# Attention and a feed-forward block on one Trainium2 core: the feed-forward by 1024 tokens, both projections by a 26-product scheme, weight forms made during attention

## The chip, the cores and the metric

One core of one Trainium2 chip runs the whole program in a single launch. The metric is the device time of that launch in microseconds (us). A run differs from the next by some tenths of a us, so about 0.2% (2 us) is what a measurement of this kernel can tell from no change.

## The reference, cut to what matters

```python
# q, k, v: (4, 8, 768, 64) float32; centroids: (8, 16, 64)
q_assign = argmax(normalised q @ normalised centroids.T)   # per head; the same for k
mask     = q_assign[..., :, None] == k_assign[..., None, :]
scores   = where(mask, q @ k.T / 8, -1e9)
x        = softmax(scores) @ v                             # -> (3072 tokens, 512)
h        = x @ w_in                                        # w_in (512, 2048)
g        = h * erf(softplus(h))
out      = g @ w_out                                       # w_out (2048, 512), all float32
```

## The kernel before, in words

**Attention** goes by 16 *periods*, one for each pair of heads of a batch entry. `period(p, i)` is one of six steps of period `p`; it handles two *units*, a unit being one block of 128 keys against one half (384) of the queries of both heads. `InOrder` keeps every engine's instructions in the order in which the program writes them, so what stands in the text first runs first on its engine.

In each step PE computes, for a unit half a period ahead, the scores from which the row maxima are taken (`maxima_step`: tile `wide`, the only one of its kind, filled by `kv,qv` and `km,qm`); DVE reduces it to `nmx` and so frees it. PE computes the scores proper into `sc`, ACT turns them into `pr` by an exponential, PE multiplies `pr` by v into `turned` (`attend`), and POOL adds the `pr` of one half up (`accumulate`, tile `more_out`, 128x768; five adds per half). At the steps 0 and 3 the half before is finished (`divide`): PE multiplies the sum by `minus`, ACT takes its inverse, DVE scales and writes a piece of x, and SP's queue stores it to `x_dram`. DVE also transposes q and k (`transposes`: k after step 2, q after step 5) and chooses the clusters (`choose`).

Beside that the weights pass through: 32 pieces of 128x512 are loaded (`fetch`) and rebuilt by ACT (`size`, `rest`, `sign`), DVE (`bounded`, `shifted`) and POOL (`summed`); 22 of them during periods 0 to 11, 10 *late* ones in the feed-forward. The same list runs in `period`: where `FORMS` says so, DVE takes a weight form (a sum or difference of two blocks of a weight, 128x512), and POOL one at steps 1 and 4 of periods 12 to 15.

```python
FORMS = {12: {0: 1}, 13: {0: 1}, 14: {0: 1, 3: 1}, 15: {0: 1, 3: 2, 4: 2, 5: 2}}
POOL_FORMS = range(12, 16)
```

**The feed-forward** goes by chunks of 512 tokens, six of them. `hidden` computes h for half of the hidden features at a time by a scheme with 7 products in place of 8 (`block`: each product is two matmuls of 128x128 by 128x256 into one of eight PSUM tiles, `bank` or `turned`; DVE and ACT add it to its places in `g`). The gate is Softplus and Erf on ACT and a product on DVE. The first chunk's out-projection (`project`) has 7 products as well; in the five others (`project26`) it has 26 products of four matmuls in place of 32, with forms of w_out that POOL makes once (`EARLY_FORMS`, `LATE_FORMS`), 10 of which lie in DRAM and are streamed through a ring of three tiles. The forms of x for the next chunk (`right_forms`) are made by DVE.

Of the kernel before, what the change touches and what calls it, by code (L numbers as in the profile page):

```python
# [19 lines left out]
P = 128  # L20
# [15 lines left out]
HT, HK, HF, HM = CT // 2, DM // P // 2, NFT // 2, DM // 2  # L36
FG = HF // 2
# [4 lines left out]
FORMS = {12: {0: 1}, 13: {0: 1}, 14: {0: 1, 3: 1}, 15: {0: 1, 3: 2, 4: 2, 5: 2}}  # L42
POOL_FORMS = range(12, 16)
# [9 lines left out]
KAPPA = {1: (0, 1), 2: (0, 0), 0: (1, 1), 3: (1, 0)}  # L53
EARLY_FORMS = [
    (-6, -4, -6, -1, None), (11, -2, -8, -1, None), (1, -3, -5, -1, None), (2, -6, 1, 1, None),
    (0, -4, 11, -1, 7), (8, -7, 11, -1, 8), (9, -5, -6, -1, 3), (11, -2, 11, 1, 10),
    (8, -7, 11, -1, 11), (6, -1, -5, 1, 1), (9, -1, 8, 1, 9), (8, 1, 11, -1, 4),
]
LATE_FORMS = [
    (3, -6, 0, -1, None), (4, 0, 6, -1, None), (0, -7, 0, 1, 6), (7, -3, 0, -1, None),  # L60
    (10, -4, 2, -1, 0), (6, -6, 6, -1, None), (9, -2, 6, 1, 2), (8, -7, 1, -1, 5),
]
HOME = (4, 0, 2, 3, 1, 5)
LAG = 1
RIGHT = [
    2, 7, -3, 100, -6, 3, 101, 4, -1, 102, 6, 103, 0,
    104, -4, -7, 105, 1, 106, 5, 107, -1, 108, -2, -2, 109,
]
# [5 lines left out]
    (-3, 16, 2, 10, 1), (-3, 17, 9, 16, 1), (-1, 18, 1, 17, 1), (2, 17, 6, 14, -1), (3, 6, 5, 6, 1),  # L74
# [35 lines left out]
N_STREAM = 10  # L110
RING = 3
KEPT = {0: 10, 5: 11}
HELD = 11
# [19 lines left out]
def kernel(  # L133
# [28 lines left out]
    more_in = const.tile([P, 3, HK, DFF // 2], F32, name="more_in")  # L162
    more_out = const.tile([P, 3, HF, HM], F32, name="more_out")
    x_more = const.tile([P, 3, HK, HT], F32, name="x_more")
    minus = const.tile([P, Q], F32, name="minus")
    alleps = const.tile([P, 1], F32, name="alleps")
    x_dram = dram.tile([DM, B * S], F32, name="x_dram")

# [30 lines left out]
    def part_of(i, lo, n):  # L199
        return more_out[:, i].rearrange("p f m -> p (f m)")[:, lo : lo + n]  # L200
# [78 lines left out]
    for f in range(HF):  # L279
        for g in (f, HF + f):  # L280
            w_steps.append((w_out[:, g], moe_w_out[g * P : (g + 1) * P]))
# [337 lines left out]
    def left_forms(engine, a11, a12, a21, a22, new):  # L619

        return [
            functools.partial(plus_of, new[0], a21, a22, engine),
            functools.partial(minus_of, new[1], new[0], a11, engine),
            functools.partial(minus_of, a21, a11, a21, engine),
            functools.partial(minus_of, new[2], a12, new[1], engine),
        ]

    def right_forms(engine, b11, b12, b21, b22, new):

        return [  # L630
            functools.partial(minus_of, new[0], b12, b11, engine),
            functools.partial(minus_of, new[1], b22, new[0], engine),
            functools.partial(minus_of, b12, b22, b12, engine),
            functools.partial(minus_of, new[2], new[1], b21, engine),
        ]

    def lefts(a11, a12, a21, a22, new):
        return {1: a11, 2: a12, 3: new[2], 4: a22, 5: new[0], 6: new[1], 7: a21}

    def rights(b11, b12, b21, b22, new):  # L640
        return {1: b11, 2: b21, 3: b22, 4: new[2], 5: new[0], 6: new[1], 7: b12}

    def w_in_parts(f, n):
        c1, c2 = slice(f * P, (f + n) * P), slice((HF + f) * P, (HF + f + n) * P)
        return (
            w_in[:, 0:HK, c1], w_in[:, HK:, c1], w_in[:, 0:HK, c2], w_in[:, HK:, c2],
            [more_in[:, i, :, c1] for i in range(3)],
        )

    def x_parts(n):  # L650
        x = x_of[n]
        return (
            x[:, 0:HK, 0:HT], x[:, 0:HK, HT:], x[:, HK:, 0:HT], x[:, HK:, HT:],
            [x_more[:, i] for i in range(3)],
        )

    def w_out_parts(f, n):
        f1, f2 = slice(f, f + n), slice(HF + f, HF + f + n)
        return (
            w_out[:, f1, 0:HM], w_out[:, f1, HM:], w_out[:, f2, 0:HM], w_out[:, f2, HM:],  # L660
            [more_out[:, i, f1] for i in range(3)],
        )

    g_of = {}
    sums_of = {}

    def g_parts(n, s, lot):
        g, new = g_of[n, s, lot], sums_of[n, s, lot]
        return (
            g[:, 0, :, 0:P], g[:, 1, :, 0:P], g[:, 0, :, P:], g[:, 1, :, P:],  # L670
            [new[:, i] for i in range(3)],
        )

    ORDER = (1, 2, 6, 7, 5, 3, 4)
    aside_work = []
    n_banks = [0]
    banks = [None]

    def bank():
        n_banks[0] += 1  # L680
        b = banks[n_banks[0] % len(banks)]
        if b is None:
            b = psb.tile([P, 512], F32, name="bank")
        return b[:, 0:HT]

    def onto(out, m, engine=ve):
        plus_of(out, m, out, engine)

    def fresh(c11, c12, c21, c22, first=ae.copy):
        return {  # L690
            1: [lambda m: first(out=c12, in_=m)],
            2: [lambda m: plus_of(c11, m, c12)],
            6: [lambda m: onto(c12, m)],
            7: [lambda m: plus_of(c21, m, c12)],
            5: [lambda m: onto(c12, m), lambda m: plus_of(c22, m, c21)],
            3: [lambda m: onto(c12, m)],
            4: [lambda m: minus_of(c21, c21, m)],
        }

    def further(c11, c12, c21, c22, u):  # L700
        return {
            1: [lambda m: ae.copy(out=u, in_=m), lambda m: onto(c11, m)],
            2: [lambda m: onto(c11, m)],
            6: [lambda m: onto(u, m), lambda m: onto(c12, u)],
            7: [lambda m: onto(u, m), lambda m: onto(c21, u)],
            5: [lambda m: onto(c12, m), lambda m: onto(u, m), lambda m: onto(c22, u)],
            3: [lambda m: onto(c12, m)],
            4: [lambda m: minus_of(c21, c21, m)],
        }

    def block(pieces, after, done=lambda i: None, pace=1):

        for i in ORDER:
            m = bank()
            pairs_of = pieces(i)
            for k, (lhsT, rhs) in enumerate(pairs_of):
                te.matmul(m, lhsT=lhsT, rhs=rhs, start=(k == 0), stop=(k == len(pairs_of) - 1))
            for f in after[i]:
                f(m)
            done(i)  # L720
            for work in aside_work[:pace]:
                work()
            del aside_work[:pace]

    def finish_aside():
        for work in aside_work:
            work()
        aside_work.clear()

    def hidden(n, lot, between={}, pace=1, **kw):  # L730

        for s in range(2):
            g_of[n, s, lot] = gp.tile([P, 2, FG, HT], F32, name="g")
        x = rights(*x_parts(n))
        for j in range(FG):
            w = lefts(*w_in_parts(lot * FG + j, 1))
            a, b = (g_of[n, s, lot] for s in range(2))
            block(
                lambda i: [(w[i][:, k], x[i][:, k]) for k in range(HK)],
                fresh(a[:, 0, j], b[:, 0, j], a[:, 1, j], b[:, 1, j], **kw), pace=pace,  # L740
            )
            between.get(j, lambda: None)()

    def gate(n, lot, s):

        g = g_of[n, s, lot].rearrange("p h j t -> p (h j t)")
        box = []

        def curves():
            t = actp.tile([P, 2 * FG * HT], F32, name="a_s")  # L750
            box.append(t)
            ae.activation(out=t, in_=g, func=ACT.Softplus)
            ae.activation(out=t, in_=t, func=ACT.Erf)

        def product(i):
            c = slice(i * 512, (i + 1) * 512)
            ve.tensor_tensor(out=g[:, c], in0=box[0][:, c], in1=g[:, c], op=ALU.mult)

        return curves, [functools.partial(product, i) for i in range(2 * FG * HT // 512)]

    def add_hidden(n, lot, s):
        sums_of[n, s, lot] = gsp.tile([P, 3, FG, P], F32, name="g_more")
        return left_forms(ve, *g_parts(n, s, lot))

    def idle(n):
        return [lambda: None] * n

    def gates(n, lot, which=(0, 1), between=()):
        work = list(between)
        for s in which:  # L770
            curves, products_of = gate(n, lot, s)
            if s == which[0]:
                work = [curves] + work + idle(7 - len(work)) + products_of
            else:
                work += [curves, *sums, *idle(3)] + products_of
            sums = add_hidden(n, lot, s)
        return work + sums
# [536 lines left out]
```

## Time and profile before

| what | value |
|---|---|
| three timed runs | 977.44, 977.89 and 978.01 us; median 977.89 |
| profiled execution, first to last instruction | 976.0 us; no time of its own is given beside the span, so the 1.9 us around it are taken from the median |
| granted TensorE clock | 1.000 |
| PE / PEld / DVE / ACT / POOL busy | 99% / 74% / 78% / 54% / 42% |
| 302 to 408 us (periods 12 to 15): PE, DVE, POOL busy of 106 | 106.0, 85.4, 89.2 us |
| 408 to 560 us (first of the feed-forward): PE, DVE, ACT, POOL busy of 151.9 | 151.9, 125.1, 77.0, 95.9 us |
| 560 to 976 us: PE, DVE, ACT, POOL busy of 416 | 411.9, 290.6, 162.0, 0 us |
| DMA | 88.4 MB, 91 GB/s in the mean |

How to read it: the span is cut by engine. PE is TensorE's matmuls and PEld its weight loads, DVE is VectorE, ACT ScalarE, POOL GpSimd, SP the queue that issues DMAs. All instructions but a few carry the line of one helper (L124), so groups are told apart by tiles (output<-inputs) and shapes. A number in square brackets behind a row is idle time of the engine before it, with what ended it. In the chain of work that ended last each row is a start, a length, an engine and how many instructions. An f32 matmul leaves two records.

### The profile page before, as it was taken

The numbers are of one execution on the slowest core, as the hardware profiler recorded it, in microseconds if no ns is written. First come the engines' busy times: TensorE is split into PE (matmuls) and PEld (weight loads), VectorE is DVE, ScalarE is ACT, GpSimd is POOL, SyncE is SP. The second block draws the span as 40 slices with busy tenths as digits, with TensorE's granted clock in tenths as the row PEclk, the third lists the DMA queues.
The fourth block names the chain that finished last, engine by engine and source line by source line (L and its number), as shares of the span: only waits on it lengthen the run. The fifth ranks groups of instructions, "written<-read, shape, count | busy, mean of one in ns | idle before, by whom it ended". The sixth has DMA issues, their size and how long they took to land.

```text
span 976.0 us, 20840 instructions
## 1 busy us (share of the span) xinstructions
PE 967.6 (99%) x8282; PEld 723.8 (74%) x8282; DVE 758.8 (78%) x1432; ACT 526.7 (54%) x799; POOL 410.0 (42%) x277
## 2 busy tenths in 40 slices
PE   8999999999999999999999999999999999999998
PEld 3555555555555555688888888888888888888887
DVE  8888888888888886879788786568666856685766
ACT  3777777777777665377613430562155235413541
POOL 1688887788888888853199600000000000000000
PEclk9999999999999999999999999999999999999999
DMA  9444444444444211142004543023302320131023
GB/s 226 74 109 110 108 110 109 107 110 109 87 110 110 54 35 34 50 149 87 0 22 173 194 147 135 1 65 130 108 0 87 130 87 1 65 139 57 1 86 108
DMA packets 157185, 88.42 MB, mean 91 GB/s; under 512 B 129696, under 2 KB 139424, under 8 KB 157088
## 3 DMA queue, kind: packets, MB, share of 16 engines
q1 hardware_dynamic: 154592, 86.67, 31.5%
q8 instruction: 65, 1.06, 0.4%
q10 hardware_dynamic: 2496, 0.43, 0.2%
q14 instruction: 32, 0.26, 0.1%
HBM read 68.19 MB, written 18.87 MB: 89 GB/s over the span
## 4 chain that ended last, share of the span: by engine, by line
PE 97%; DVE 2%; DMA 0%; issue 0%; ACT 0%; DVEq 0%; SPq 0%
PE bank L124 43%; PE turned L124 32%; PE sc L124 17%; PE wide L124 6%; DVE nmx L124 1%; DMA in_q<-in_q_dram 0%; DVE kT L124 0%; DVE sims L124 0%; DVE qT L124 0%; DVE km L124 0%; DVE turned L124 0%; DVE nbig L124 0%; ACT qm L124 0%; DVE ccT L124 0%; DVE osb L124 0%
## 5 line engine op out<-in xcount | busy, mean ns | idle before, releaser
L124 POOL TENSOR_TENSOR more_out<-more_out,pr 128x768 f32<-128x768 f32 x128 | 217.2, 1697 | 18.5 <-ACT pr L124 10.0
L124 DVE TENSOR_REDUCE nmx<-wide 128x2 f32<-128x768 f32 x189 | 180.5, 955 | 47.8 <-PE wide L124 47.0
L124 ACT ACTIVATE pr<-sc 128x768 f32<-128x768 f32 x192 | 148.7, 810 | 94.1 <-PE wide L124 77.2
L124 PE MATMUL turned<-pr,in_v 128*32 128x193 f32 x3072 | 144.8, 330 | 0.0
L124 DVE TENSOR_TENSOR g<-bank,g 128x256 f32<-128x256 f32 x222 | 89.4, 419 | 54.2 <-PE bank L124 34.1
L124 PEld LDWEIGHTS turned<-pr,in_v 128*32 128x32 f32 x3072 | 91.5, 109 | 50.7 <-issue 21.3
L124 DVE TENSOR_TENSOR g<-g 128x512 f32<-128x512 f32 x114 | 78.9, 692 | 42.3 <-PE bank L124 32.2
L124 PE MATMUL bank<-x_own,w_in 128*128 128x256 f32 x424 | 104.5, 379 | 0.0
L124 PE MATMUL sc<-qT,kT 64*128 64x384 f32 x528 | 98.3, 486 | 0.0
L124 PEld LDWEIGHTS bank<-x_own,w_in 128*128 128x128 f32 x424 | 80.4, 190 | 11.5 <-issue 0.6
L124 ACT ACT_TABLE_LOAD x48 | 61.6, 1283 | 38.2 <-DVE g L124 37.5
L124 DVE TENSOR_TENSOR g<-a_s,g 128x512 f32<-128x512 f32 x96 | 74.1, 786 | 3.2 <-ACT a_s L124 3.2
L124 PE MATMUL bank<-x_more,more_in 128*128 128x256 f32 x296 | 76.0, 379 | 0.0
L124 PE MATMUL bank<-w_out,g 128*128 128x256 f32 x328 | 75.7, 379 | 0.0
L124 POOL TENSOR_TENSOR more_out<-pr,pr 128x768 f32<-128x768 f32 x32 | 60.3, 1886 | 28.3 <-ACT pr L124 28.3
L124 PE MATMUL bank<-g_more,g 128*128 128x256 f32 x296 | 69.9, 379 | 0.0
L124 PEld LDWEIGHTS bank<-w_out,g 128*128 128x128 f32 x328 | 62.2, 190 | 8.6
L124 PEld LDWEIGHTS <-qv 64*128 64x128 bf16 x384 | 27.0, 93 | 52.9 <-issue 36.7
L124 PEld LDWEIGHTS sc<-qT,kT 64*128 64x128 f32 x528 | 50.0, 187 | 21.4 <-ACT inv L124 2.4
L124 PE MATMUL wide<-kv,qv 64*128 64x384 bf16 x378 | 64.0, 328 | 1.3 <-DVE nmx L124 0.6
L124 PE MATMUL wide<-km,qm 64*128 64x384 bf16 (+1 forms) x378 | 62.6, 327 | 0.0
L124 PEld LDWEIGHTS bank<-g_more,g 128*128 128x128 f32 x296 | 56.2, 190 | 7.6
(195 smaller groups left out, 1745.6 us busy)
## 6 DMA issues: line engine op xcount, KB each, us to landing
g_more<-b_dram SPq DMA_DIRECT2D x48, 512.0 KB, 3.2
x_own<-in_moe_w_in_dram SPq DMA_DIRECT2D x13, 512.0 KB, 4.1
in_v<-in_v_dram SPq DMA_DIRECT2D x32, 192.0 KB, 3.1
x_dram<-more_out SPq DMA_DIRECT2D x128, 48.0 KB, 1.8
x_own<-x_dram SPq DMA_DIRECT2D x6, 1024.0 KB, 5.5
in_k<-in_k_dram SPq DMA_DIRECT2D x59, 96.0 KB, 2.6
in_q<-in_q_dram SPq DMA_DIRECT2D x58, 96.0 KB, 2.6
out_dram<-osb SPq DMA_DIRECT2D x20, 256.0 KB, 3.2
```

The costliest lines, as they stand in the source:

```text
L124: ins = getattr(self.engine, name)(*args, **kw)
```

## The change

The feed-forward goes by 1024 tokens, three times. Each of the two projections is 26 products of eight matmuls (128x128 by 128x256). One product of `hidden` fills two PSUM banks (128x1024), and three such tiles are in use in turn; adds, copies and gate steps go by 128x1024. The list `HIDDEN` gives the products of the in-projection in order: the form or raw block of w_in, the form of x, and what is done with the result (an entry of one number is a copy on ACT, one of four an add on DVE, with -1 for the product itself).

The 18 forms of w_in are made during attention in two pieces of 128x512 each, in turn by DVE and POOL (`FORMS_VE`, `FORMS_GE`: period, then steps), and each is stored to DRAM; six raw blocks are stored too. In the feed-forward the blocks come back through a ring of five tiles in order of use; the place of w_in holds blocks of h then. The forms of x are made by POOL (`X_FORMS`: the first number is the product behind which it is issued, negative ones in the round before). The ten late weight pieces are spread over products 0 to 14 of the first round (`LATE_STEPS`), and the 18 forms of w_out are made by POOL there, behind the products that `OUT_MADE` names (26 and more are products of the out-projection); ten of them are stored and streamed in the later rounds. `SOFT`, `ERF` and `TIMES` place the gate.

```diff
-FORMS = {12: {0: 1}, 13: {0: 1}, 14: {0: 1, 3: 1}, 15: {0: 1, 3: 2, 4: 2, 5: 2}}
-POOL_FORMS = range(12, 16)
+W_FORMS = [
+    (17, -3, -5, -1, 4), (11, -6, -5, -1, 0), (6, -1, -5, 1, 3), (10, -6, 6, -1, 2), (9, -2, 10, 1, 1),
...
+W_RAW = {5: (0, 1), 7: (2, 3), 9: (5, 6)}
+FORMS_VE = {
+    9: {1: 1, 2: 1}, 10: {1: 1, 2: 1}, 11: {1: 1, 2: 1}, 12: {1: 1, 2: 1}, 13: {1: 1, 2: 1},
+    14: {1: 1, 2: 1, 3: 1, 4: 1}, 15: {0: 1, 1: 1, 2: 1, 3: 1, 4: 1, 5: 1},
+}
+FORMS_GE = {9: (0, 3), 10: (0, 3), 11: (0, 3), 12: (0, 1, 3, 4), 13: (0, 1, 3, 4), 14: (0, 1, 3, 4), 15: (0, 1, 3, 4)}
...
+X_FORMS = [
+    (-3, 0, 2, 4, -1), (-1, 1, 7, 1, 1), (-1, 2, 5, -2, -1), (2, 3, 7, 6, 1), (3, 2, -1, -2, -1), (4, 1, -2, 6, 1),
+    (5, 4, 5, 4, 1), (7, 2, -2, 0, 1), (9, 0, 5, -1, -1), (10, 1, 3, -1, -1), (11, 2, 0, 4, -1), (12, 3, 7, 3, 1),
+    (12, 4, -3, -4, -1), (14, 0, -3, 6, 1), (15, 1, -4, 6, 1), (16, 4, -2, 2, 1), (19, 0, -3, 5, -1), (20, 1, -1, 1, 1),
+]
+HIDDEN = [
+    (25, -1, [(0,)]),
+    (-2, 3, [(1,)]),
...
+    (-4, 1, [(13,), (9, 9, -1, -1), (14, 9, 3, -1), (9, 6, 9, 1), (12, 12, 9, -1), (3, 9, 3, -1)]),
+    (13, -1, [(15, -1, 10, -1), (8, 8, 15, -1)]),
...
+    (10, -5, [(18, -1, 17, -1)]),
...
+    (7, -2, [(6, -1, 6, -1), (18, 6, 18, -1)]),
...
+OUT_MADE = {
+    14: [17], 16: [22], 18: [18], 19: [0], 22: [1], 23: [3], 25: [20], 26: [5], 27: [6], 28: [7], 29: [10],
+    30: [9], 31: [11], 32: [12], 33: [19], 34: [13], 35: [25], 36: [16],
+}
+LATE_STEPS = {0: 0, 1: 1, 3: 2, 4: 3, 6: 4, 7: 5, 9: 6, 10: 7, 12: 8, 13: 9}
+LANDING = (17, 18, 15, 16)
+SOFT = {7: (4, 8), 13: (3, 15), 14: (11, 7), 18: (0, 12), 21: (5, 6), 22: (14, 1), 25: (10, 2), 29: (9, 13)}
+ERF = {8: (4, 8), 15: (3, 15), 16: (11, 7), 19: (0, 12), 23: (5, 6), 24: (14, 1), 26: (10, 2), 30: (9, 13)}
...
+    def w_form(form, i, engine):
+        o, a, b, sign, at = form
+        signed(sign, engine, w_piece(o, i), w_piece(a, i), w_piece(b, i))
+        if i:
+            nc.sync.dma_start(out=w_dram[w_at[o]], in_=more_in[:, at])
...
+    def make_out_form(x):
+        a, b, sign = OUT_FORMS[x]
+        for f in (0, 2):
+            signed(sign, ge, *(out_form(i)[:, f : f + 2] for i in (x, a, b)))
+        if x in OUT_STREAM:
+            nc.sync.dma_start(out=b_dram[OUT_STREAM.index(x)], in_=more_in[:, items.index((0, x, 1)) % RING])
...
+    def weights(i):
+        n = {at: N_EARLY + k for at, k in LATE_STEPS.items()}
+        if i in n:
+            size_and_rest(n[i])
+            bounded(n[i])
+        if i - 1 in n:
+            sign(n[i - 1])
+            shifted(n[i - 1])
+            summed(n[i - 1])
+
+    def hidden(n, between={}):
+        for i, (w, x, ops) in enumerate(HIDDEN):
+            m = product()
+            rows = m.rearrange("p a (b t) -> p (a b) t", b=2)
+            wt, xt = ring(w, 0), x_at(n, x)
+            for j in range(FT):
+                for k in range(KT):
+                    te.matmul(
+                        rows[:, j], lhsT=wt[:, k * CT + j * P : k * CT + (j + 1) * P], rhs=xt[:, k],
+                        start=(k == 0), stop=(k == KT - 1),
+                    )
+            if HIDDEN[i + 1 : i + 2] == [] or HIDDEN[i + 1][0] != w:
+                fill(item[0] + RING)
...
+            for op in ops:
+                if len(op) == 1:
+                    ae.copy(out=bufs[op[0]], in_=m)
+                else:
+                    o, a, b, sign = op
+                    signed(sign, ve, of(o), of(a), of(b))
+            x_forms(n, i, i + 1)
+            gate(i)
+            gated(i)
+            if n == 0:
+                weights(i)
+                for x in OUT_MADE.get(i, ()):
+                    make_out_form(x)
+            left_step(i - len(HIDDEN))
...
-        for _ in range(min(len(forms), FORMS.get(p, {}).get(i, 0))):
+        for _ in range(min(len(forms), FORMS_VE.get(p, {}).get(i, 0))):
             forms.pop(0)[0]()
...
-            if i % HJ == 1 and p in POOL_FORMS and forms:
+            if i in FORMS_GE.get(p, ()) and forms:
                 forms.pop(0)[1]()
...
+    psb = pool("psb", 3, space=PSUM)
...
+    for n in range(NS):
+        hidden(n, {1: lambda: run(last)} if n == 0 else {})
+        project(n)
```

## The prediction

> **What bounds the kernel now.** I read the page's shares and its chain, then the windows, then the chain over 640 to 700 us.
>
> ```profile
> PE 967.6 (99%) x8282; PEld 723.8 (74%) x8282; DVE 758.8 (78%) x1432; ACT 526.7 (54%) x799; POOL 410.0 (42%) x277
> ...
> PE 97%; DVE 2%; DMA 0%; issue 0%; ACT 0%; DVEq 0%; SPq 0%
> ```
>
> PE is busy and on the chain from end to end, so time is gained only by fewer PE instructions and lost wherever PE is made to wait.
>
> ```profile
> 649.04 10.36 PE bank L124 x48
> 659.40 3.45 PE turned L124 x16
> ```
>
> An f32 matmul leaves two records, so 10.36 us is 24 matmuls: 0.432 us each. The ffn has 1304 of them (counted below); 1304 x 0.432 = 563, and PE takes 563.8 us for it, from 408.1 (its first ffn product) to 971.9. There is no gap to win, only products.
>
> In attention PE is also full, and DVE is just behind it. Around step i = 1 of period 12, DVE first, then PE:
>
> ```profile
> 317.09 0.96 DVE L124 TENSOR_REDUCE nmx<-wide 128x2 f32<-128x768 f32 x1
> ...
> 319.89 0.54 DVE L124 SCALAR_TENSOR_TENSOR more_out<-den,turned 128x384 f32<-128x384 f32 x1
> 320.85 0.96 DVE L124 TENSOR_REDUCE nmx<-wide 128x2 f32<-128x768 f32 x1 [0.42 <-PE wide L124]
> 322.77 0.96 DVE L124 TENSOR_REDUCE nmx<-wide 128x2 f32<-128x768 f32 x1 [0.96 <-PE wide L124]
> 323.77 0.19 DVE L124 TENSOR_REDUCE lowest<-nmx 128x6 bf16<-128x18 f32 x1
> ```
> ```profile
> 318.18 0.33 PE L124 MATMUL wide<-kv,qv 64*128 64x384 bf16 x2
> ...
> 321.94 0.48 PE L124 MATMUL wide<-kv,qv 64*128 64x384 bf16 x2
> ```
>
> There is one `wide` tile. PE refills it at 318.18 and 321.94, 0.13 us after `nmx` has emptied it (318.05, 321.81). So 0.13 us is all the room; what DVE is later than that at the first `nmx` of a step, PE loses.
>
> What DVE pays for an add of two SBUF tiles depends on POOL:
>
> ```profile
> 316.39 0.68 DVE L124 TENSOR_TENSOR more_in<-w_in 128x512 f32<-128x512 f32 x1
> ...
> 403.68 2.16 DVE L124 TENSOR_TENSOR more_in<-w_in,more_in 128x512 f32<-128x512 f32 x1
> 405.77 2.17 DVE L124 TENSOR_TENSOR x_more<-x_own,x_more 128x512 f32<-128x512 f32 x1
> ```
> ```profile
> 403.16 8.40 POOL L124 TENSOR_TENSOR more_out<-more_out,pr 128x768 f32<-128x768 f32 x4
> ```
>
> Same shape: 0.68 us with POOL waiting, 2.16 with POOL accumulating; POOL's sums slow from 1.72 to 2.10. They take turns. From 500 to 530 us, POOL busy throughout:
>
> ```profile
> L124 DVE TENSOR_TENSOR g<-a_s,g 128x512 f32<-128x512 f32 x8 | 10.3, 1292 | 1.1 <-ACT a_s L124 1.1
> ...
> L124 DVE TENSOR_TENSOR g<-bank,g 128x256 f32<-128x256 f32 x5 | 2.0, 413 | 0.1
> ```
>
> With a PSUM operand (`bank`) nothing is added; with two SBUF operands 0.61 us over the 0.68.
>
> **The change, part by part** (against the profiled span, 976.0; the median is 1.9 us above it).
>
> *PE.* In-projection: 6 chunks x 2 x 4 x 7 x 2 = 672 matmuls become 3 x 26 x 8 = 624. Out: 112 + 5 x 104 = 632 become 3 x 26 x 8 = 624. 56 fewer, same shape: -24.2 us.
>
> *Weight forms in attention.* 36 half forms of 128x512 replace 20. DVE gets 16: after steps 1 and 2 of periods 9 to 13, 1 to 4 of 14, 0 and 1 of 15. DVE runs in order and `nmx` is queued behind each, PE behind `nmx`. So a piece costs its duration less DVE's idle time before that `nmx` (0.25 us at step 1 in periods 9 to 11, 0.42 in 12 and 13, none at step 2, where the transpose of k fills it) less 0.13.
> - Periods 9 to 11: at step 1 POOL's sum ends 0.1 us after the piece is reached (270.00 + 1.84 against 271.74): 0.78 - 0.38 = 0.40. At step 2 it falls in the third sum, 0.35 us before its end: 1.03 - 0.13 = 0.90. POOL's new piece at step 3 meets DVE's weight preparation: 0.5. Together 1.8 x 3 = 5.4.
> - Periods 12, 13: at 320.43 POOL is in a sum until 321.5, 1.68 - 0.55 = 1.13; at step 2 (323.96) a sum has started 0.2 us before, 2.1 - 0.13 = 1.97. Together 3.1 x 2 = 6.2.
> - Periods 14, 15 (no transposes or routing, so more idle): between 0.4 and 7.9 by the same formula with 0.68 and 2.17; I take 4.0, the middle.
>
> Sum 15.6. If every piece finds POOL idle: 4.4. If every one takes 2.17, with 3 for the preparation: 30. A gain is excluded: work put ahead of `nmx` brings nothing forward.
>
> Trainium skill, SBUF — State Buffer, "Who interferes with whom": the pair of ports that DVE and GpSimd share is an exclusive lock, and the later one blocks for the whole instruction. By it a piece could cost 0.68 + 1.72 = 2.40, 0.23 above the dearest row; for this term 2 to 4 us more. The rows decide.
>
> *POOL in attention.* 20 pieces of 1.27 us where it had 8. Five sums are 8.7 us of the 12.2 of a half period; two pieces make 11.3. The cover is that PE reads the sums 0.8 us after the last (316.11 against 315.32): 0, at most 0.3 for each of 8 halves if that is gone.
>
> *Stores.* 24 of 512 KB on SP's queue, where one row lands in 3.2 us. Queued behind are loads for the next period and x, 10 us and more early: 0. The streamed blocks (35 per 1024 tokens, 18 MB in some 180 us, 100 GB/s where slices of the page show 194) start five items, 14 us, ahead: 0.
>
> *First 1024 tokens: ACT.* A product lasts 8 x 0.432 = 3.45 us. During products 7 to 14 ACT has 6 copies and 8 curves of 128x1024 (1.05 each, the `a_s` row), 3 table loads (1.28), and for late weights 5 size-and-rest and 6 signs (1.36 each): 14.7 + 3.8 + 15.0 = 33.5 us in 27.6. POOL's `summed` waits for `sign`; behind it in POOL's queue stand the x forms that PE needs. Walking the queues from the first product: sign(5) ends at 40.9, `summed` 42.2, the x form 43.5, product 12 was due at 41.9: 1.5. `bounded` and `shifted` hold DVE behind ACT until 52, so the pair of forms after `summed`(7) is ready at 57.7 for product 15, due at 53.9: 3.8. sign(9) at 67.2, sum, one out form (2.5), x form at 72.3 for product 18, due 68.0: 4.3. Sum 9.6. Low end 3.8 (the last alone); high 15, if DVE's sums meet POOL each time.
>
> *First 1024 tokens: DVE against POOL.* From product 16 to 25 DVE has 30 ops of 128x1024; from 0.42 and 0.69 for 256 and 512 columns one is 1.23, overlapped about 1.15: 34.5 us for 34.5 us of PE. No room is left, and the last left operand for the out-projection is finished just as it is wanted. By product 23, 15 of them have two SBUF tiles, and POOL is busy some 31 of 52 us there: 15 x 0.61 x 0.6 = 5.5; I take 5.0. Low 0, high 13 (all wait, more until product 36).
>
> *The other 2048 tokens.* POOL has only 18 x forms each time; three fall into products 16 to 20: 3 x 0.61 at most, 0.75 taken, twice: 1.5 (0 to 5). ACT is below half there: 0. The end (two half products, as before one): 0, within 1.
>
> 976.0 - 24.2 + 15.6 + 9.6 + 5.0 + 1.5 = 983.5; with 1.9, **985.4**.
>
> **Rivals.**
> *Lock found free (faster).* The two DVE terms depend on which moment of POOL's cycle each piece meets. At their low ends (4.4, 0, 0.5) with ACT's 9.6 the time is 977.9 - 24.2 + 14.5 = 968.2. For it: rows at 316.39 with 0.68. Against: at steps 1 and 2 POOL's sums run nearly gapless. It decides below a mean of about 0.9 us for a DVE form piece: every 0.1 us is 1.6 us of time, and the change of sign needs some 7.
>
> *Pure arithmetic (faster).* Three PSUM tiles and the five-item ring take up everything: 953.7. Against it: ACT's 33.5 us in 27.6.
>
> *Form making becomes the bound (slower still).* From product 16 to 36 of the first round out forms, x forms and two-tile adds share one lane; turn by turn they need some 61 us in the first 52, PE stands for most of the 10, and attention is nearer to its high end: 1000 and more.
>
> *The streams are not hidden*, because fills stand behind a store that waits for POOL: 5 to 10 us in the first round; seen as waits of PEld on DMA.
>
> **How the numbers follow.** Forecast (978 to 997): 0.46; form making the bound: 0.12; streams: 0.02; lock free: 0.24; pure arithmetic: 0.10; within 0.2% (2 us, about what this measurement can tell): 0.06. Faster is 0.34, slower 0.60. The range takes in the lock-free case and most of the arithmetic one below, and form making to 1006 above; about one in ten is left on each side. The likeliest case's own range is 978 to 997.
>
> **What would show it.** Right: ffn products still 0.432 us each and 1248 of them; period length, now 24.45 us (277.93 to 302.38 in the chain), 26 to 28 in periods 9 to 14, with waits of PE `wide` on DVE `nmx` of over 10 us in sum where there are 0.6 now; DVE form pieces of 1 to 2.2 us; PE gaps in the first ffn round before products 12, 15 and 18, released by POOL's x forms; none in the second and third. Wrong: periods of 24.5 us, form pieces of 0.7, an ffn of 540 us. If POOL shows sums of the accumulators late at the divisions, its term was not 0.

## The result and the profile after: 1006.17 us, slower by 2.9%

The changed kernel takes 1006.17 us in the median of four runs (1004.73 to 1006.43), against 977.77 us before (977.44 to 978.01, four runs): ratio 1.0287, 95% interval 1.0272 to 1.0302. The profiled execution is the one of 1004.73 us, with a span of 1003.0 us and a mean granted TensorE clock of 0.988. The forecast was 985.4, slower by 0.8%, and its range ended at 1006.

The page after: busy time and count by engine, the granted clock by slice of 25 us, and the shares of the chain that ended last.

```profile
PE 959.3 (96%) x8170; PEld 708.9 (71%) x8170; DVE 774.0 (77%) x956; ACT 540.5 (54%) x746; POOL 500.7 (50%) x322
...
PEclk9999999999999999999889999999999999999999
...
PE 74%; DVE 19%; issue 3%; ACT 1%; DMA 1%; SPq 1%; POOL 0%; DVEq 0%; POOLq 0%
```

PE is busy for only 8.3 us less, although 56 matmuls of 0.432 us (24.2 us) have gone: some of those that are left run at a lower clock (10.8 us of it, below). Its share of the chain fell from 97% to 74%: DVE now holds the path for 19%.

The feed-forward goes three times over the same products; these three passes are called rounds. The chain over 640 to 720 us, in the second round (start, length, what):

```profile
639.88 51.37 PE product L178 x238
691.25 0.24 issue
```

238 records are 119 matmuls of 0.432 us, with 0.24 us lost between them. Here the change does what it says.

The span, cut at the first ffn product, at the first product of the second round and at the end of the last product. The first column of numbers is measured in the kernel before for the attention and the end; for the rounds it counts products of the new kernel without a gap:

| stage | before, or all products without a gap | after | more |
|---|---|---|---|
| attention, to the first ffn product | 408.07 | 422.70 | +14.6 |
| first round, 52 products of 3.456 us | 179.7 | 216.6 | +36.9 |
| second and third round, 832 matmuls | 359.4 | 360.3 | +0.9 |
| end, after the last product | 4.1 | 3.5 | -0.6 |

Attention. DVE and then PE around step 2 of period 12, as the lines of before from 317 to 324:

```profile
324.43 0.95 DVE L178 TENSOR_REDUCE nmx<-wide 128x2 f32<-128x768 f32 x1
325.29 0.54 DVE L178 SCALAR_TENSOR_TENSOR more_out<-den,turned 128x384 f32<-128x384 f32 x1
325.75 1.71 DVE L178 TENSOR_TENSOR more_in<-more_in,w_in 128x512 f32<-128x512 f32 x1
327.38 0.95 DVE L178 TENSOR_REDUCE nmx<-wide 128x2 f32<-128x768 f32 x1
...
330.16 2.12 DVE L178 TENSOR_TENSOR more_in<-more_in,w_in 128x512 f32<-128x512 f32 x1
```
```profile
328.38 0.34 PE L178 MATMUL wide<-kv,qv 64*128 64x384 bf16 x2 [0.73 <-DVE nmx L178]
```

The piece after step 1 takes 1.71 us and the next `nmx` stands behind it; PE refills `wide` 0.05 us after that `nmx` (327.38 + 0.95) and had waited 0.73 us. The piece after step 2 takes 2.12.

First round. PE's gaps (in brackets, with their releaser), from two windows of one view:

```profile
467.46 7.17 PE L178 MATMUL product<-x_more,more_in 128*128 128x256 f32 x32 [2.39 <-POOL x_more L178]
475.41 3.72 PE L178 MATMUL product<-x_more,more_in 128*128 128x256 f32 x16 [0.78 <-POOL x_more L178]
484.28 9.99 PE L178 MATMUL product<-more_in 128*128 128x256 f32 x32 [5.16 <-POOL more_in L178]
501.04 6.69 PE L178 MATMUL product<-x_more,more_in 128*128 128x256 f32 x16 [3.31 <-POOL x_more L178]
...
525.00 6.64 PE L178 MATMUL product<-x_more,more_in 128*128 128x256 f32 x16 [3.46 <-POOL more_in L178]
...
574.97 5.38 PE L178 MATMUL product<-more_in,h 128*128 128x256 f32 x16 [2.39 <-DVE h L178]
```

The gaps before products 12, 15 and 18 end with an x form of POOL (a form of x, which PE multiplies by), as foreseen, and so does a small one before product 14. The one before product 23 (525.00) is put down to POOL too, but its PSUM tile came free only at 524.74, by an add of DVE; those that follow name DVE. The chain of work agrees: from 504 to 545 us it runs on DVE, but for some 4 us that the profile puts down to no engine. And there is something that the prediction did not count: behind a gap of 3.3 us or more, the first 16 records take some 6.6 us in place of 3.6. The granted clock from 501 to 508 us is 0.57, from 525 to 531.5 it is 0.54. All gaps of the round are 22.9 us in sum, and the products behind four of them are 10.8 us longer than at full clock.

### The profile page after: what moved, and what is told of

It reads as the page before. It is cut to its first block, busy times and chain, and to the rows that moved or that the text cites. A ratio compares the mean times of both kernels' runs of the same rounds, so it can differ in the third digit from the quotient of the medians.

```text
span 1003.0 us, 19956 instructions
## 1 busy us (share of the span) xinstructions
PE 959.3 (96%) x8170; PEld 708.9 (71%) x8170; DVE 774.0 (77%) x956; ACT 540.5 (54%) x746; POOL 500.7 (50%) x322
## 4 chain that ended last, share of the span: by engine, by line
PE 74%; DVE 19%; issue 3%; ACT 1%; DMA 1%; SPq 1%; POOL 0%; DVEq 0%; POOLq 0%
PE product L178 43%; PE turned L178 13%; PE sc L178 13%; DVE h L178 5%; PE wide L178 5%; DVE nmx L178 4%; DVE w_in L178 4%; DVE more_in L178 2%; DMA x_dram<-more_out 1%; DVE w_out L178 1%; DVE more_out L178 1%; DVE c L178 1%; DVE kT L178 0%; DVE turned L178 0%; ACT a L178 0%
## 5 line engine op out<-in xcount | busy, mean ns | idle before, releaser
L178 PE MATMUL product<-x_more,more_in 128*128 128x256 f32 x624 | 145.1, 391 | 9.9 <-POOL x_more L178 6.5
L178 PEld LDWEIGHTS product<-x_more,more_in 128*128 128x128 f32 x624 | 122.3, 197 | 29.6 <-POOL x_more L178 8.0
L178 PE MATMUL product<-w_out,h 128*128 128x256 f32 x384 | 86.3, 379 | 0.0
L178 PE MATMUL product<-x_own,more_in 128*128 128x256 f32 x384 | 85.8, 379 | 0.0
L178 PE MATMUL product<-more_in,h 128*128 128x256 f32 x336 | 77.5, 386 | 5.0 <-DVE h L178 2.6
L178 PEld LDWEIGHTS product<-x_own,more_in 128*128 128x128 f32 x384 | 73.0, 190 | 9.9
L178 PEld LDWEIGHTS product<-w_out,h 128*128 128x128 f32 x384 | 73.0, 190 | 9.9
L178 DVE TENSOR_TENSOR h<-h,h 128x1024 f32<-128x1024 f32 x45 | 69.0, 1540 | 12.2 <-PE product L178 11.4
L178 PEld LDWEIGHTS product<-more_in,h 128*128 128x128 f32 x336 | 64.8, 193 | 15.1 <-issue 6.1
L178 DVE TENSOR_TENSOR h<-h,product 128x1024 f32<-128x1024 f32 x24 | 28.9, 1216 | 57.2 <-ACT h L178 35.0
```

Source lines behind the costliest of these rows:

```text
L178: ins = getattr(self.engine, name)(*args, **kw)
```

## Experiments

Ten kernels ran, each edited from the changed one. "First product" is the first ffn product (after: 422.70 us), "round" the length of the first round (after: 216.6, gapless 179.7). Times are medians beside 977.7 us for before.

### DVE's form pieces left out

```diff
...
-            forms.pop(0)[0]()
+            forms.pop(0)[2]()     # the store of a finished block only
...
+            if i == 2 and 2 <= p <= 7:
+                ge.memset(more_in[:, p - 2], 0.0)
```

> Leaves out the 16 pieces of w_in forms that DVE makes in attention (POOL's 20 pieces, all stores and loads stay; the blocks hold zeros or partial forms). Theory (DVE pieces stand ahead of nmx, and PE waits for nmx): the first halves of periods 9 to 15 lose their 1.8 us each, the first ffn product moves from 422.8 to 409 to 412 us, the whole to 990.5 to 994 us; what stays (about 3 us in the second halves of periods 12 to 15) is POOL's. Rival (POOL's 20 pieces, or the stores on SP's queue, delay attention): the first ffn product stays at 419 us or later.

997.89 us. First product at 414.14. The zeros, which POOL writes in periods 2 to 7 into `more_in`, cost 3.6 us themselves (the `lowest` of period 7 comes at 204.74, after: 201.11), which the expectation had missed; without them it would be 410.5: 12.2 us less, as the theory said. By half periods, from one `lowest` (a DVE step that comes once in a half) to the next: with a piece after step 2 14.16 us in periods 12 and 13, without it 12.42 and 12.41. What POOL's pieces cost is 0.64 in each of periods 9 to 11 (the piece after step 3) and 0.2 at most later, not the 3 us in periods 12 to 15 that were expected. The whole missed its range by the zeros and by a round 1.6 us longer.

### Pieces moved to where they cost least

```diff
-FORMS_VE = {9: {1: 1, 2: 1}, ..., 14: {1: 1, 2: 1, 3: 1, 4: 1}, 15: {0: 1, ..., 5: 1}}
-FORMS_GE = {9: (0, 3), 10: (0, 3), 11: (0, 3), 12: (0, 1, 3, 4), ...}
+FORMS_VE = {7: {1: 1}, ..., 11: {1: 1}, 12: {0: 1}, 13: {0: 1}, 14: {0: 1, 3: 1}, 15: {0: 1, 3: 2, 4: 2}}
+FORMS_GE = {6: (0,), ..., 11: (0,), 12: (0, 1, 3, 4), ..., 15: (0, 1, 3, 4)}
```

> Same work, other places in attention only: POOL makes 22 pieces of w_in forms (from period 6 on, after step 0, and after 0, 1, 3, 4 in periods 12 to 15), DVE 14 at the places that cost nothing or least in the trace (after step 1 in periods 7 to 11, after step 0 in 12 to 15, after 3 and 4 of 14 and 15); none after step 2. Theory (what a piece costs is its time ahead of nmx, 1.2 to 1.8 us after step 2 and 0.1 after step 1 of the periods before 12; POOL's pieces cost 0.6 at step 3 where weights are rebuilt and nothing in periods 12 to 15): the first ffn product at 409 to 411 us in place of 422.8, the whole 992.5 to 995. Rival (the number of pieces counts, wherever they stand, since POOL and DVE share a lane): the first product at 417 or later, 1000 or more.

994.59 us, first product at 411.82, 2.0 of which are a wait for POOL's first x form, late behind its sums: the last `lowest` came at 397.64 (before: 395.98, after: 410.67). All 36 pieces are there; their places, with two of them moved from DVE to POOL, made 10.9 of the 14.6 us.

### The rebuilding of late weights left out

```diff
...
         if i in n:
-            size_and_rest(n[i])
-            bounded(n[i])
+            pass
-        if i - 1 in n:
-            sign(n[i - 1])
-            shifted(n[i - 1])
-            summed(n[i - 1])
+        if i - 1 in n and n[i - 1] in after_of:
+            fetch(after_of[n[i - 1]])
...
```

> Leaves out the rebuilding of the ten late weight pieces in the first ffn round on ACT, DVE and POOL (their loads stay; w_out is 0 there). Theory (POOL's x forms stand behind sums that wait for ACT's sign): the PE gaps before products 12, 14, 15 and 18 (2.4, 0.8, 5.2, 3.3 us) and the two half-clock stretches behind them (3.1 us each) go: 18 us less, about 987. Rival (DVE is the bound from product 16 on, whatever ACT and POOL do before): the gaps move to products 20 and later, and no more than 7 us is gained, 998 or more.

992.41 us; the round is 199.7, 16.9 shorter, near the theory's 18 (zeros written by POOL in attention cost 4.2 on the other side). Of the four gaps before products 12 to 18 only 1.19 us is left, so the late weights were their cause: their work on ACT, DVE and POOL together, which this run doesn't tell apart. The rival had a part: DVE's gaps stay, with a new one of 5.06 at out-product 0.

### The forms of w_out left out

```diff
-        for f in (0, 2):
-            signed(sign, ge, *(out_form(i)[:, f : f + 2] for i in (x, a, b)))
```

> Leaves out POOL's 36 halves of w_out forms in the first ffn round (stores and streams stay). Theory (DVE's adds of two SBUF tiles wait for POOL, 1.21 us becoming 2.2): DVE's 128x1024 adds stay near 1.2 to 1.4 us, the PE gaps from product 23 to product 12 of the out-projection (11.4 us in sum) and the half-clock stretches behind two of them (4.8 us) go: 15 to 16 us less, about 990; the gaps before products 12, 14 and 15 stay, that before 18 falls by 1 to 2. Rival (DVE has too much work even alone): its adds get shorter, but the gaps stay above half of their sum, 998 or more.

984.83 us; the round is 196.3, 20.3 shorter, more than the theory's 16. After out-product 0 no gap is left, and DVE's adds of two SBUF tiles are short, as the theory said: from 500 to 600 us their mean is 1.30 us (47 instructions of 128x1024), where the changed kernel has 1.90 (40). One of their groups (after the bar: busy us, mean ns of one, idle before):

```profile
L178 DVE TENSOR_TENSOR h<-h,w_in 128x1024 f32<-128x1024 f32 x7 | 8.6, 1221 | 2.3 <-PE product L178 2.2
```

With the run before, 16.9 + 20.3 = 37.2, which is about the whole of the 36.9. No run leaves out both, and both shorten the stretch at product 18, so the two numbers need not add up.

### PE kept busy in the gaps

```diff
+FILL = {12: 3, 15: 8, 18: 8, 23: 8, 32: 3, 35: 5, 38: 4}
...
+    def keep_busy(i):
+        for _ in range(FILL.get(i, 0)):
+            te.matmul(turned[1][:, 0:TB], lhsT=w_out[:, 0, 0:P], rhs=w_out[:, 0, 0:TB], start=True, stop=True)
...
```

> Adds 39 f32 matmuls of 128x128 by 128x256 into an idle PSUM bank ahead of products 12 (3), 15 (8), 18 (8), 23 (8) and of out-products 6 (3), 9 (5) and 12 (4) of the first round, so that no idle time of PE is over 2.5 us; no other change. Theory A (the half-clock stretches after the gaps, 11 us in sum, are on the path that sets the end): clock of 0.95 or more in every slice, the first round 8 to 11 us shorter in spite of 17 us more of PE work, about 995. Theory B (ACT and DVE are late anyway, and PE's slow products only fill time in which it would wait): full clock, but the gaps before products 18 and later get longer by what the products save; 0 to 4 us less, 1001 to 1006.

1005.56 us; round 217.6. PE's rows (the fillers are `turned<-w_out`):

```profile
484.18 7.17 PE L179 MATMUL product<-more_in 128*128 128x256 f32 x32 [1.71 <-POOL more_in L179]
491.19 3.62 PE L179 MATMUL product<-x_more,more_in 128*128 128x256 f32 x16
494.65 3.62 PE L179 MATMUL turned<-w_out 128*128 128x256 f32 x16
500.94 6.76 PE L179 MATMUL product<-x_more,more_in 128*128 128x256 f32 x16 [2.68 <-POOL x_more L179]
```

Product 15 and the next now run at full clock (7.17 us for what took 9.99), and product 18 starts at 500.94 where it started at 501.04. The 2.8 us that PE saved became more waiting and filling. Product 23 runs at full clock too, and the next late one, out-product 0, starts no earlier: at 540.59, behind a wait of 5.09 for DVE, in place of 538.70 without fillers. So theory B holds where this run can tell: there the slow clock is a mark of the gaps and no cause of time. It can't tell at product 18, which stayed slow (2.68 us of idleness was enough), nor at out-products 6, 9 and 12, where the fillers fill the whole gap and may have held the product themselves. In sum the products behind gaps were 11 us longer than at full clock, and the run got 0.6 back.

The Trainium skill, TensorE: Matmul & The Clock Gate, "What's actually happening", says that an idle window of about 3.4 us, free-running, halves the clock until about as long a time of work has passed. The rows agree in kind: behind gaps the clock fell to 0.54 to 0.57 for some 6.5 us, and the length of a gap alone doesn't decide (2.39 us did not lower it at 467.46, and did at 574.97, where it is 0.72 from 575 to 581 us). In size they differ: 2.39, 2.68 and 3.31 us are shorter than that window and lowered it, and the measurement decides.

### No table switch for Softplus

```diff
...
-            ae.activation(out=scratch[SCRATCH[s]], in_=slot(s), func=ACT.Softplus)
+            ae.activation(out=scratch[SCRATCH[s]], in_=slot(s), func=ACT.Erf if early[0] and i < 18 else ACT.Softplus)
...
```

> The eight Softplus curves of the first 18 products of the first round (all rounds after stay) are computed as Erf instead: as long, another function, and ACT needs no table load between them, Erf and the rebuilding of the late weights. Theory (the table loads, 1.28 us each, that the late weights force beside Softplus make ACT's queue late, and with it POOL's sums and x forms): six or seven loads fewer, the gap before product 12 (2.4 us) goes, those before 15 and 18 fall from 8.5 to below 4, the first round 5 to 8 us shorter, 998 to 1001. Rival (ACT's order, not its load: sums, signs and x forms wait for each other in turn however fast ACT is): 0 to 2 us, 1004 to 1006.

1000.73 us; round 211.7, 4.9 shorter. From 420 to 600 us there are 9 table loads in place of 16 (a table load, 1.28 us, stands where ACT goes over to certain other functions); the gap before product 12 is gone, those before 15 and 18 stay at 5.13 and 2.25, not below 4 in sum as expected. So theory and measurement meet only at the theory's low end: 4.9 of the 16.9 us hang on these seven loads. That the rest is the order (POOL's sum waits for `sign`, the x form for the sum) follows from the program and is not shown by a run of its own. ACT's rows in the changed kernel show where the uncounted loads come from:

```profile
453.61 2.00 ACT L178 ACTIVATE a<-h 128x1024 f32<-128x1024 f32 x2
455.63 1.28 ACT L178 ACT_TABLE_LOAD   x1
456.93 0.67 ACT L178 ACTIVATE w_out<-w_in 128x512 f32<-128x512 f32 x1
```

Behind two Softplus curves (`a<-h`) a late piece's `size` (`w_out<-w_in`) needs another table.

### The forms of w_out by DVE

```diff
-        for f in (0, 2):
-            signed(sign, ge, *(out_form(i)[:, f : f + 2] for i in (x, a, b)))
+        signed(sign, ve, *(out_form(i) for i in (x, a, b)))
```

> One edit to the changed kernel: the 18 w_out forms are made by DVE, as whole 128x1024 blocks at the same places of the program, instead of by POOL in halves. DVE gets 18 x 1.22 = 22 us of work, POOL loses 36 x 1.27 = 46. Theory (a POOL half beside DVE's adds of two SBUF tiles costs DVE about 1.05, so that POOL's forms cost a full DVE up to 36 us, more than making them itself): adds of DVE back at 1.2, the gaps from product 23 on smaller by a third to a half, 996 to 1001. Rival (DVE is full by its own instructions and any work added to it shows in full): 22 us of added work, of which at most 5 fall into idle time, 1015 or more.

996.40 us; round 207.6, 9.0 shorter, although DVE, the late engine, got 22 us more to do. The gaps from product 23 on fell less than expected, from 11.3 to 9.3 us; the gap before product 18 is 1 us shorter, and there is a new one of 1.96 before product 20, whose end the profile puts down to no engine. So the gaps are only 1.0 us shorter in sum, and the other 8 are slow products that no longer follow (from 540 on the granted clock is 1.00). In the run with fillers full clock alone brought no such gain, so it is DVE's earlier end that counts here; this is an argument from two runs. DVE's groups by shape from 500 to 600 us (after the bar: busy us, mean ns of one, idle before), after and here:

```profile
L178 DVE TENSOR_TENSOR h<-h,w_in 128x1024 f32<-128x1024 f32 x6 | 11.5, 1918 | 0.1
L178 DVE TENSOR_TENSOR w_in<-c,w_in 128x1024 f32<-128x1024 f32 x5 | 10.4, 2087 | 0.0
...
L178 DVE TENSOR_TENSOR w_in<-w_in,product 128x1024 f32<-128x1024 f32 x5 | 6.0, 1209 | 0.0
```
```profile
L178 DVE TENSOR_TENSOR h<-h,w_in 128x1024 f32<-128x1024 f32 x6 | 7.3, 1218 | 0.1
L178 DVE TENSOR_TENSOR w_in<-c,w_in 128x1024 f32<-128x1024 f32 x5 | 7.1, 1427 | 0.0
...
L178 DVE TENSOR_TENSOR w_in<-w_in,product 128x1024 f32<-128x1024 f32 x5 | 6.1, 1211 | 0.0
```

With an operand in PSUM (`product`) POOL makes no difference, 1.21 us either way; with two in SBUF, 1.9 to 2.1 fall to 1.2 to 1.4. Over all groups of that shape with two SBUF operands the mean in this window is 1.90 us (40 instructions) after, 1.30 (60, forms included) here.

The Trainium skill, SBUF — State Buffer, "Who interferes with whom", names just that: a DVE instruction with two SBUF inputs contends with a GpSimd instruction that reads SBUF, one with at most one such input, outside the two-port modes, does not. The groups agree, with 0.7 us on a 1.22 us add as the mean price.

### Three versions with all of the work

First, late weights and kept forms earlier:

```diff
...
-N_LATE = 10
-LAST_X = 11
+N_LATE = 6
+LAST_X = 13
-LATE_STEPS = {0: 0, 1: 1, 3: 2, 4: 3, 6: 4, 7: 5, 9: 6, 10: 7, 12: 8, 13: 9}
+LATE_STEPS = {0: 0, 1: 1, 2: 2, 3: 3, 4: 4, 5: 5}
...
-    14: [17], 16: [22], 18: [18], 19: [0], 22: [1], 23: [3], 25: [20], 26: [5], 27: [6], ...
+    5: [17], 6: [22], 7: [18], 8: [0], 9: [20], 13: [6], 22: [1], 23: [3], 26: [5], ...
```

> A version that keeps all of the work. As in the run with the forms moved to POOL, but four of the ten late weight pieces go into periods 12 and 13 of attention (x is loaded after period 13 in place of 11), the other six stand at products 0 to 5, ahead of the first Softplus, and the six w_out forms that stay in place are made behind products 5 to 9 and 13 in place of 14 to 27. Theory (attention loses 12 us to the place of DVE's pieces; the first round 17 to late weights that stand among Softplus and x forms and 20 to w_out forms that meet DVE's adds): attention ends at 411 to 413; no gaps of PE before product 18; half of the w_out forms no longer meet DVE, so 8 to 10 us stay after product 20; 971 to 976, faster than before. Rival (the shared lane and ACT are full however the work is ordered): 990 or more.

983.37 us, ratio 1.0053 (1.0036 to 1.0070): between theory and rival (the profiled execution took 985.03). First product at 415.81, of which 2.66 are a wait for the first x form; round 203.8. The gaps before products 10, 12 and 13 (2.44, 0.92, 0.94 us, released by x forms) are new: POOL's kept forms now stand ahead of the x forms. The largest are 4.18 and 4.56, released by DVE, in the out-projection.

Second, eleven of the w_out forms by DVE where it has little to do, five of them through c tiles and DRAM, and each x form issued as soon as its tile is free:

```diff
...
+    0: [17, 0, 3, 11], 5: [22, 18, 20], 7: [1, 16], 8: [5], 10: [6], 28: [7], 29: [10], 30: [9], ...
+OUT_VE = (17, 0, 3, 11, 22, 18, 20, 1, 16, 5, 6)
+OUT_EARLY = {3: 0, 11: 1, 1: 2, 16: 3, 5: 0}
...
```

> Keeps all of the work. Eight late weight pieces at products 0 to 7 (two more in period 12), Softplus of products 7 moved to 8; DVE, idle until product 4 and again near 8 to 10, makes eleven of the w_out forms as whole 128x1024 blocks behind products 0, 5, 7, 8 and 10, five of them through c tiles and DRAM; POOL's other seven forms start at product 28; x forms are issued as soon as their tile is free; one DVE form piece fewer in each of the last steps of period 15. Theory (what costs is POOL's 128x512 instructions beside DVE's full stretch, products 12 to 36, and x forms queued behind others): no PE gap before product 18, at most one of 2 us until out-product 0, 4 to 8 us in the out-projection; first product at 411 to 413; 966 to 972. Rival (DVE has no room anywhere once the lane is shared, 11 whole blocks move its late point forward): 980 or more.

977.77 us, ratio 1.0002 (0.9990 to 1.0013): as before, between theory and rival (the profiled execution took 979.55). First product at 415.12, later than expected, of which 2.29 are a wait for the first x form; round 197.8. The forms behind products 5 to 10 met POOL's late sums and x forms there and made DVE late for product 14 (a gap of 2.99), and POOL's last seven still met DVE in the out-projection (2.58 and 2.36).

Third, no form of w_out on POOL at all, the forms spread more evenly, and other x forms by DVE (the diff is against the second):

```diff
...
+    0: [17, 0, 3, 11], 3: [22, 18], 4: [20], 5: [1], 7: [16], 8: [5], 9: [6], 28: [7], 29: [10], ...
+    38: [19], 44: [25],
-OUT_VE = (17, 0, 3, 11, 22, 18, 20, 1, 16, 5, 6)
+OUT_VE = tuple(OUT_FORMS)
...
```

> Keeps all of the work; as the version with the forms before the rush, with these differences: six late pieces again (four in periods 12 and 13), all w_out forms by DVE, those from products 3 to 9 one or two behind a product, two of the last at out-products 12 and 18; the first x form by DVE in period 15, and the x forms for the next round by DVE. Theory (in the full stretch of DVE its own 1.22 us for a form is less than the 2.1 that POOL's two halves take from it): first product at 412.5 to 414, no gap above 1 us after it, the first round 182 to 187 us; 959 to 966, faster than before. Rival (DVE has no room left in the out-projection): gaps of 5 us and more from out-product 5 on, 972 or more.

971.07 us, ratio 0.9929 (0.9912 to 0.9946): faster than before by 0.7%, five to twelve us short of the expectation. The page:

```profile
PE 949.9 (98%) x8170; PEld 702.4 (72%) x8170; DVE 768.5 (79%) x981; ACT 534.5 (55%) x742; POOL 424.9 (44%) x279
...
PEclk9999999999999999999999999999999999999999
```

And 30 us of the out-projection in the windows view (first length, then busy us and count of PE, PEld, DVE, ACT, POOL, then clock, DMA share and GB/s), after and here:

```profile
540.00:570.00 30.00, 27.92 (x129) 24.00 (x128) 29.83 (x17) 13.16 (x15) 25.17 (x13) 1.00 0.33 123
```
```profile
540.00:570.00 30.00, 30.00 (x140) 26.41 (x139) 26.95 (x30) 6.52 (x11) 0.00 (x0) 1.00 0.34 123
```

With POOL still, DVE has 3 us to spare, and PE has no gap. That also answers the rival that three PSUM tiles are too few for this stretch: they are the same three. Several things changed at once, so the run shows that such an order exists, not what each part of it is worth. The round of 192.4 us is still 12.7 above the gapless 179.7, by gaps in its first part (the last one, 2.96 us before product 15, ends at 475.88); attention ends 4.9 late.

## Why the prediction was wrong

The direction was right, and so were most of the places and the mechanisms. Two terms of the sum, both for the first 1024 tokens, were much too small: 9.6 + 5.0 = 14.6 us where 36.9 were measured. The time fell just outside the range.

*PE, -24.2: right.* 1248 ffn products of 0.432 us.

*Weight forms in attention, 15.6: right, 14.6 measured, and mostly by its own steps.* After step 2 of periods 12 and 13 a piece cost 1.75 us in place of the 1.97 forecast, after step 1 0.9 in place of 1.13; 1.2 and 0.1 in periods 9 to 11 for 0.90 and 0.40; POOL's piece at step 3 0.64 for 0.5; those of periods 14 and 15 together 4.0 for 4.0, which is luck, since 4.0 was the middle of 0.4 to 7.9. Together 15.1, of which the periods before give 0.4 back (the `lowest` of period 7 comes at 201.11, before: 201.46). POOL's own term, 0, held in periods 12 to 15.

*First 1024 tokens, ACT, 9.6: the step that failed first.* The waits were those named (products 12, 15, 18), 11.6 us with product 14. But the time without late weights is 16.9 shorter. The term counted three table loads behind products 7 to 14; there are seven, since `size` and `sign` of a late piece after Softplus need their own, a case that before, with its Softplus elsewhere, did not show. The four that were missed are among the seven whose removal gained 4.9. The rest of the difference of 7.3, which may be the order of the queues and what DVE's `bounded` and `shifted` and POOL's sums do to later products, isn't taken apart by a run and stays open.

*First 1024 tokens, DVE against POOL, 5.0: the step that failed most, 20.3 measured.* Its form was right (two-SBUF instructions pay, PSUM ones don't), two of its three factors were low. It took 15 instructions where there were 40: the stretch doesn't end at product 23 but runs to out-product 12, since DVE, once late, stays late. And it took 0.61 us for one, from 128x512, where an overlapped 128x1024 one loses 1.0. The third factor, 0.6 of them overlapped, was about right: 26 of the 40 took 2.1 us or more. 40 x (1.90 - 1.22) = 27 us from 500 to 600 us, against 20.3 that the round lost; what absorbed the difference isn't shown. The prediction said "No room is left" in the same paragraph and yet ended the sum at product 23, as if DVE caught up there. The high end given, 13, went on to product 36, but with the same 0.61.

*The other 2048 tokens, 1.5: 0.9 measured.*

*Rivals.* "Form making becomes the bound", at a chance of 0.12, is nearest to what came in the first round: the path lay on DVE and the time was over 1000. Its other part did not come: attention was nowhere near its high end (14.6 of 30), and 16.9 us hang on the late weights. "Lock found free" and "pure arithmetic" held 0.34 together; against them the text itself had POOL's 31 of 52 us and ACT's 33.5 us in 27.6. "Streams" left no mark: no wait of PE or PEld is put down to a DMA.

## What to carry to other kernels

Where an engine has no slack, price contention per instruction of the shape at hand, and over the whole stretch until the engine has caught up: here 40 instructions at a mean of 0.7 us, not 15 at 0.4. Work that is given to an engine "because it is idle" is not free when it shares a lane with the full one: here the full engine did the same work itself for less. And a long instruction belongs where its engine idles, not ahead of a short one that somebody waits for: the same 36 pieces cost 14.6 us or, at other places and two of them on the other engine, 3.8.

## What was unexpected in the hardware

A half clock for some 6.5 us behind a gap of 5.2 us cost nothing where another engine set the pace: 2.8 us of faster products came back as 2.8 us of waiting. Six blocks of zeros, 128x1024, that POOL wrote in 0.95 us each, one a period, cost 3.6 us in attention. And the first round, with DVE on its path, ended 9.0 us sooner when DVE had 18 instructions of 1.22 us more to do and POOL 36 of 1.27 less.
